# K cache in runs of 32 KB, two heads to a tile: a change to a one-core decode kernel

## The chip, the cores and the metric

The kernel runs on one core of one Trainium2 chip. The metric is the device time of one execution in microseconds (us). A core has five engines that run side by side: TensorE (PE, with its weight loads as PEld), VectorE (DVE), ScalarE (ACT), GpSimd (POOL) and SyncE (SP). SP issues nearly all transfers here, and 16 DMA engines carry them out. On-chip memory (SBUF) has 128 partitions; matmuls write to PSUM.

## The reference

One decode step for 4 sequences (B = 4, one token each, D = 576) is the sum of the input, an attention branch and an MLP branch, both on the layer-normed input:

```
xn = layernorm(x)
out = x + A(xn) + B(xn)

A: q = xn @ wq                          # 32 query heads of 128
   k, v = the last W = 2048 positions of the caches, 16 heads of 128, each used by 2 query heads
   o = softmax(q k^T / sqrt(128)) v
   return o @ wo
B: xn + gelu(layernorm(xn) @ w3) @ w4   # F = 4608; for one token the part before it (h, w1, w2) vanishes
```

With one token, the shifts in branch B move every value out of the sequence, so `w1` and `w2` are not read. All arrays are bf16. The windows of K and V are 4 x 16 x 2048 x 128 values each, 33.55 MB, and with the weights the kernel reads 87.17 MB.

## The kernel before

**Stages.** The kernel works in one pass over its bytes. First come `wq` in five pieces and the query projection (L204), then 16 heads of K, with the five pieces of `w3` between the first of them, then the softmax, then 16 heads of V with the output projections, and at the end three quarters of `w4`.

**K.** `kv_load` (L98) fetches one head for all 4 batches as a tile of 2 MB: 128 partitions (32 blocks of 64 positions x 4 batches), 16 KB of contiguous bytes to each. The pool `kv` has 6 such tiles (`NKV`), and V uses the same pool. `k_scores` (L252) turns the tile around on DVE with two STREAM_TRANSPOSEs (L258), one for each half of the head dimension, into a tile `kt` (a pool of two), and then issues 64 small matmuls (L267), 32 on each half, which add the scores of this head for all batches into four PSUM banks S. The queries lie in `qz` with zeros around them, so that each head's scores land in rows of their own.

**Softmax.** After the last head of K, `softmax` (L273) takes the maximum on DVE (L279), Exp on ACT with four calls of 512 columns, one for each bank (L283), scales and spreads the result (L300, L302), transposes it on PE (L306) and copies it to `PZ` (L312, L314) in four pieces.

**V.** `v_compute` (L319) multiplies one head of V by its columns of `PZ` in 64 matmuls (L325). `head_out` (L342) copies the result out and puts two steps off to later rounds through the list `later`: `select` (L351), and for every second head `project`, eight matmuls with a tile of `wo` (L330). `wo` has a pool of three tiles, loaded by `load_wo` (L338).

**Order.** Each engine takes its instructions in the order written by a scheduler at build time, and waits on semaphores. SP's order decides when a transfer is queued: a transfer that waits for a free buffer holds up all that stand behind it. In the V stage SP has, in this order: V0 to V3, wo0, wo1, V4, wo2, V5, V6, wo3, V7, V8, wo4, and so on. V6 is the first that needs a V buffer back (V0's), and wo3 the first that needs a `wo` buffer back (wo0's, after its `project`). On PE the first two heads of V are computed piece by piece beside each other, as the pieces of `PZ` come; the `project` of wo0 stands behind V3.

Of the kernel before, what the change touches and what calls it, by code (L numbers as in the profile page):

```python
# [8 lines left out]
ACT = mybir.ActivationFunctionType  # L9
ALU = mybir.AluOpType  # L10
AX = mybir.AxisListType
BF16 = mybir.dt.bfloat16
F32 = mybir.dt.float32
I32 = mybir.dt.int32
PSUM = bass.MemoryType.PSUM

NKV = 6
NWP = 3


# [1 line left out]
def kernel(  # L22
# [11 lines left out]
    B_w4: bass.AP,  # L34
    out: bass.AP,
):

    nc = tc.nc
    P = 128
    B, Sq, D = A_x.shape
    _, Hkv, Sk, Dh = A_k_cache.shape
    Hq = A_wq.shape[1] // Dh
    rep = Hq // Hkv
    W = min(4096, max(256, Sk // 4))
    F = B_w3.shape[1]
    assert Sq == 1 and Dh == P and rep == 2 and B == 4 and W == 2048
    assert D == 576 and F % (2 * P) == 0 and Hkv * rep == 32 and Hkv % 2 == 0  # L50
    G = 32
    NCH = W // G
    NG = P // G
    GK = G // B
    NY = 4
# [3 lines left out]
    KJ = 4  # L59
# [4 lines left out]
    scale = float(Dh) ** -0.5  # L64
# [6 lines left out]
    k_win = A_k_cache[:, :, Sk - W:Sk, :]  # L71
    v_win = A_v_cache[:, :, Sk - W:Sk, :]

    def ap_of(t, offset_elems, dims):
        a = t[:]
        return bass.AP(a.tensor, a.offset + offset_elems, [list(a.ap[0])] + [list(d) for d in dims])

    def ap32(t, offset, dims):
        a = t[:].rearrange("p a b -> p (a b)") if len(t.shape) == 3 else t[:].rearrange("p a b c d e -> p (a b c d e)")
        a = a.bitcast(I32)  # L80
        return bass.AP(a.tensor, a.offset + offset, [list(a.ap[0])] + [list(d) for d in dims])

    const = ctx.enter_context(tc.tile_pool(name="const", bufs=1))
    small = ctx.enter_context(tc.tile_pool(name="small", bufs=2))
    kvp = ctx.enter_context(tc.tile_pool(name="kv", bufs=NKV))
    ktp = ctx.enter_context(tc.tile_pool(name="kt", bufs=2))
# [8 lines left out]
    x_bf = const.tile([B, D], BF16)  # L95
    nc.scalar.dma_start(out=x_bf[:], in_=x2)

    def kv_load(win, h):  # L98
        t = kvp.tile([P, NCH, Dh], BF16, tag="kv")
        nc.sync.dma_start(out=t[:].rearrange("p c d -> p (c d)"),  # L100
                          in_=win[:, h].rearrange("b (p c) d -> p b (c d)", p=G))
        return t

    wq_src = A_wq[0:KJ * P, :].rearrange("(p j) n -> p j n", j=KJ)
    w3_src = B_w3[0:KJ * P, :].rearrange("(p j) f -> p j f", j=KJ)
# [4 lines left out]
    def load_rows(src, j, n, name):  # L110
        t = wpl.tile([P, n], BF16, tag="w", name=name)
        nc.sync.dma_start(out=t[:], in_=src[:, j, :])
        return t

    def load_tail(w, n, name):
        t = wpl.tile([P, n // 2], BF16, tag="w", name=name)
        nc.sync.dma_start(out=t[:], in_=w[KJ * P:D, :].rearrange("r (e f) -> (r e) f", e=2))
        return t
# [89 lines left out]
    for j in range(KJ):  # L208
        q_piece(wq_j[j], j)
        if len(wq_j) < KJ:  # L210
            wq_j.append(load_rows(wq_src, len(wq_j), NQ, f"wq{len(wq_j)}"))
    K_tiles = {0: kv_load(k_win, 0)}
    V_tiles = {}

    q_rows = ktp.tile([P, 2, HB, NY, NG, G], BF16, tag="kt", name="q_rows")
# [33 lines left out]

    S = []  # L250

    def k_scores(h):  # L252

        kn = K_tiles.pop(h)

        kt = ktp.tile([P, NCH // 2, 2, G, 2, 2], BF16, tag="kt", name=f"kt{h}")
        for e in range(2):
            nc.vector.transpose(  # L258
                out=ap32(kt, e * G * 2, [[2 * G * 2, NCH // 2], [1, 2], [2, G]]),
                in_=ap32(kn, e * G, [[2 * 2 * G, NCH // 2], [2 * G, 2], [1, G]]))  # L260
        if h == 0:
            S.extend(ps_s.tile([P, 512], F32, tag="S", name=f"S{g}") for g in range(NG))
        for y in range(NY):
            e, t = divmod(y, 2)
            for b in range(B):
                for g in range(NG):
                    nc.tensor.matmul(out=S[g][32 * b:32 * b + 32, :].rearrange("p (c k l) -> p c k l", k=GK, l=2),  # L267
                                     lhsT=qz[32 * g:32 * g + 32, b, h, y, :],
                                     rhs=kt[32 * g:32 * g + 32, :, e, b:G:B, :, t],
                                     start=(h == 0 and y == 0), stop=(h == Hkv - 1 and y == NY - 1),  # L270
                                     skip_group_check=True)

    def softmax():  # L273
        E = wpl.tile([P, NCH, NG, GK], F32, tag="w", name="E")
        mx = const.tile([P, NG], F32)
        nb = const.tile([P, 1], F32)
        sm = const.tile([P, NG], F32)
        for g in range(NG):
            nc.vector.reduce_max(out=mx[:, g:g + 1], in_=S[g][:], axis=AX.X)  # L279
        nc.vector.reduce_max(out=nb[:], in_=mx[:], axis=AX.X)  # L280
        nc.vector.tensor_scalar_mul(out=nb[:], in0=nb[:], scalar1=-scale)  # L281
        for g in range(NG):
            nc.scalar.activation(out=E[:, :, g, :].rearrange("p (c l) k -> p c k l", l=2),  # L283
                                 in_=S[g][:].rearrange("p (c k l) -> p c k l", k=GK, l=2), func=ACT.Exp, bias=nb[:], scale=scale, accum_out=sm[:, g:g + 1])
        rd = const.tile([P, 1], F32)
        nc.vector.tensor_reduce(out=rd[:], in_=sm[:], op=ALU.add, axis=AX.X)
        nc.vector.reciprocal(out=rd[:], in_=rd[:])
        rdm = const.tile([P, B], F32)
        nc.vector.tensor_scalar_mul(out=rdm[:], in0=mask[:], scalar1=rd[:])  # L289

        PZ = pzp.tile([P, NCH, P], BF16, tag="pz", name="PZ")
        HC = CP // 2
        for piece in range(NP):
            c0 = piece * CP
            pr = ktp.tile([P, CP, NG, GK, B], BF16, tag="kt", name=f"pr{piece}")
            for b in range(B):
                src = E[:, c0:c0 + CP, :, :].rearrange("p c g k -> p (c g k)")
                dst = pr[:, :, :, :, b].rearrange("p c g k -> p (c g k)")
                if b == 3 or (b == 1 and piece % 2):
                    nc.scalar.mul(out=dst, in_=src, mul=rdm[:, b:b + 1])  # L300
                else:
                    nc.vector.tensor_scalar_mul(out=dst, in0=src, scalar1=rdm[:, b:b + 1])  # L302
            for half in range(2):
                tp = ps_s.tile([P, HC, P], BF16, tag="S", name=f"pt{piece}{half}")
                for cc in range(HC):
                    nc.tensor.transpose(out=tp[:, cc, :],  # L306
                                        in_=pr[:, half * HC + cc, :, :, :].rearrange("p g k b -> p (g k b)"),
                                        identity=ident[:])
                dst = PZ[:, c0 + half * HC:c0 + (half + 1) * HC, :].rearrange("p c n -> p (c n)")
                src = tp[:].rearrange("p c n -> p (c n)")  # L310
                if half:
                    nc.scalar.copy(out=dst, in_=src)  # L312
                else:
                    nc.vector.tensor_copy(out=dst.bitcast(I32), in_=src.bitcast(I32))  # L314
        return PZ
# [3 lines left out]
    def v_compute(h):  # L319
        bank = ps_o.tile([P, 128], F32, tag="O", name=f"O{h}")  # L320
        O = bank[:, 0:B * rep].rearrange("p (b r) -> p b r", r=rep)
        O_tiles[h] = (O, bank[:, 64:64 + XR * rep * B].rearrange("p (x n) -> p x n", x=XR))
        vn = V_tiles.pop(h)
        for c in range(NCH):
            nc.tensor.matmul(out=O, lhsT=vn[:, c, :], rhs=PZ[:, c, :].rearrange("p (b n) -> p b n", b=B)[:, :, h * rep:(h + 1) * rep],  # L325
                             start=(c == 0), stop=(c == NCH - 1))

    def acc_matmuls(lhsT, rhs_cols):
# [47 lines left out]
    def g_piece(t, j):  # L376
        for fc in range(NF):
            e, i = divmod(fc, NFH)
            if j < KJ:
                lhsT, rhs = t[:, e * (F // 2) + i:(e + 1) * (F // 2):NFH], ln2T[:, j, :]  # L380
            else:
                lhsT, rhs = t[:, i:F // 2:NFH], ln2T[:, KJ + e, :]
            nc.tensor.matmul(out=gp[:, fc, :], lhsT=lhsT, rhs=rhs, start=False, stop=False, skip_group_check=True)  # L383
# [26 lines left out]


    w3 = {}
    for h in range(Hkv):
        if h > 0:
            K_tiles[h] = kv_load(k_win, h)
        if h < KJ:
            w3[h] = load_rows(w3_src, h, F, f"w3_{h}")
        elif h == KJ:
            w3[KJ] = load_tail(B_w3, F, "w3_t")
        k_scores(h)  # L420
        if h in w3:
            g_piece(w3.pop(h), h)
            if h == KJ:
                gelu()


    NV0 = 4
    w4 = load_w4(0, 0, 9, (9,))
    for v in range(NV0):
        V_tiles[v] = kv_load(v_win, v)  # L430
    for g2 in range(2):
        load_wo(g2)
    mlp_out(*w4[0])
# [1 line left out]
    for v in range(Hkv):  # L435
        n = v + NV0
        if n < Hkv:
            V_tiles[n] = kv_load(v_win, n)
            if n % 2 == 0:
                load_wo(n // 2)  # L440
        run_later()
        v_compute(v)
        head_out(v)
# [4 lines left out]
        run_later()  # L448
    for part in end[1:]:
        mlp_out(*part)  # L450
    assert not K_tiles and not V_tiles and not wo_tiles

    fin = const.tile([P, DH], out.dtype)
    NR = 32 + B
# [33 lines left out]
```

## Time and profile before

| What | Value |
|---|---|
| Median of 3 runs | 218.01 us (217.16 to 218.03) |
| Profiled execution, own time | 217.48 us |
| Its span, first to last instruction | 215.6 us |
| Busy: PE, DVE, ACT | 115.0, 108.9, 21.1 us |
| Bytes moved | 87.52 MB, mean 406 GB/s |
| DMA packets | 8255 |
| K: 16 transfers of 2048 KB, issue to landing | 24.7 us (median) |
| V: 16 transfers of 2048 KB, issue to landing | 29.3 us (median) |

The span is what lies between the first and the last instruction of the profiled execution; its own time is 1.9 us longer. A group line of the profile has the source line, the engine, the operation, the tiles written and read, their shapes and the count, then after the first bar the busy time and the mean of one in ns, and after the second the engine's idle time just before these instructions and what ended it. In the row of 40 slices each digit is the busy share in tenths of one 40th of the span. A window line has start and end, its length, the busy time and count of PE, PEld, DVE, ACT and POOL, the granted TensorE clock, the DMA share and GB/s. A line of the chain of waits has start, length and what the chain went through, and a line of SP's waits has total, times and longest.

### The profile page before, as it was taken

To read this page: it belongs to the slowest core of one execution; us is meant where nothing else is said; L and a number is where in the kernel's file an instruction comes from. 1 tells how busy PE (TensorE), PEld (TensorE's weight loads), DVE (VectorE), ACT (ScalarE), POOL (GpSimd) and SP (SyncE) were. 2 spreads that over 40 slices of the span, in tenths; PEclk is the share of its full clock that TensorE was granted. 3 is DMA by queue.
4 is the path that set the end of the run, shared out by engine and by line. 5 is a ranking of instruction groups with operands and counts; after the bars stand their busy time and mean duration, and the time that the engine had idled before them with its cause. 6 is when DMAs were issued, how large, how long until landed. Compare 5 with 4: busy or idle time off the path is not lost.

```text
span 215.6 us, 5534 instructions
## 1 busy us (share of the span) xinstructions
PE 115.0 (53%) x2577; PEld 74.3 (34%) x2577; DVE 108.9 (51%) x156; ACT 21.1 (10%) x36; POOL 1.8 (1%) x8
## 2 busy tenths in 40 slices
PE   0343788748644554445424098748662634536383
PEld 0110744426311111111101087747452434434341
DVE  7932967584999999989785592201100000001000
ACT  0202220000000000000003896100000000000000
POOL 1110000000000000000000000000000000000000
PEclk9999999658767667558588557555555555555559
DMA  6999999999999999999999999999999999999970
GB/s 259 432 418 442 413 436 433 405 439 407 433 426 432 417 423 429 426 429 432 410 438 417 435 411 428 428 417 389 417 430 420 418 433 420 429 422 423 422 288 18
DMA packets 8255, 87.52 MB, mean 406 GB/s; under 512 B 925, under 2 KB 1065, under 8 KB 2729
## 3 DMA queue, kind: packets, MB, share of 16 engines
q1 hardware_dynamic: 8216, 87.17, 96.1%
q8 instruction: 20, 0.33, 0.6%
q14 instruction: 3, 0.02, 0.0%
q10 hardware_dynamic: 16, 0.01, 0.0%
HBM read 87.17 MB, written 0.00 MB: 404 GB/s over the span
## 4 chain that ended last, share of the span: by engine, by line
DMA 70%; DVE 13%; PE 8%; ACT 5%; issue 2%; SPq 1%; DVEq 0%; ACTq 0%
DMA t<-in_A_k_cache_dram 36%; DMA t<-in_A_v_cache_dram 21%; DMA w<-in_B_w_dram 9%; DVE kt L258 6%; DMA wq<-in_A_wq_dram 3%; PE pt L306 3%; PE O L325 2%; ACT E L283 2%; DVE qz L177 2%; PE qp L204 1%; ACT PZ L312 1%; ACT pr L300 1%; DVE mx L279 1%; DVE pr L302 1%; PE ACC L330 1%
## 5 line engine op out<-in xcount | busy, mean ns | idle before, releaser
L258 DVE STREAM_TRANSPOSE kt<-t 128x2048 int32<-128x2048 int32 x32 | 72.3, 2292 | 12.8 <-DMA t<-in_A_k_cache_dram 12.8
L267 PE MATMUL S<-kt,qz 32*32 32x512 bf16 x1024 | 36.9, 625 | 38.0 <-DVE kt L258 36.6
L325 PE MATMUL O<-PZ,t 128*128 128x8 bf16 x1024 | 30.3, 168 | 26.2 <-DMA t<-in_A_v_cache_dram 22.6
L325 PEld LDWEIGHTS <-t 128*128 128x128 bf16 x1024 | 29.0, 104 | 30.2 <-DMA t<-in_A_v_cache_dram 25.2
L347 DVE CAST on<-O 128x8 bf16<-128x8 f32 x16 | 2.7, 167 | 57.9 <-PE O L325 57.8
L267 PEld LDWEIGHTS <-qz 32*32 32x32 bf16 x1024 | 10.8, 94 | 60.6 <-issue 57.4
L306 PE MATMUL pt<-ident,pr 128*128 128x128 bf16 x64 | 6.7, 292 | 9.4 <-DVE pr L302 8.2
L383 PEld LDWEIGHTS <-w 128*128 128x128 bf16 x144 | 9.2, 162 | 5.2 <-DMA w<-in_B_w_dram 2.7
L383 PE MATMUL ACC<-ln2T,w 128*128 128x4 bf16 x144 | 9.6, 202 | 1.7 <-DMA w<-in_B_w_dram 1.7
L330 PE MATMUL ACC<-wo,onx 128*4 128x288 bf16 x64 | 9.0, 436 | 2.2 <-DVE onx L359 2.2
L283 ACT ACTIVATE E<-S,nb 128x512 f32<-128x512 f32 x4 | 4.0, 1115 | 59.5 <-DVE nb L281 59.5
L306 PEld LDWEIGHTS <-pr 128*128 128x128 bf16 x64 | 5.9, 135 | 10.0 <-ACT pr L300 10.0
L300 ACT ACTIVATE pr<-E,rdm 128x512 bf16<-128x512 f32 x6 | 8.1, 1430 | 0.8 <-DVE rdm L289 0.8
L359 DVE CAST onx<-O 32x16 bf16<-32x16 f32 x32 | 5.3, 165 | 5.3 <-PE O L351 4.9
L330 PE MATMUL ACC<-w,gT 128*4 128x288 bf16 x72 | 7.5, 368 | 0.8 <-DMA w<-in_B_w_dram 0.7
L302 DVE TENSOR_SCALAR pr<-E,rdm 128x512 bf16<-128x512 f32 x10 | 6.5, 809 | 0.3 <-PE pt L306 0.2
L204 PE MATMUL qp<-wq,xnT 128*4 128x512 bf16 x32 | 4.0, 620 | 4.5 <-DMA wq<-in_A_wq_dram 4.5
L224 DVE CAST q_rows<-qp 128x256 bf16<-128x256 f32 x8 | 2.9, 410 | 6.4 <-PE qp L204 6.4
L351 PE MATMUL O<-on,ident 128*32 128x8 bf16 x64 | 4.1, 171 | 3.6 <-DVE on L347 3.6
L351 PEld LDWEIGHTS <-ident 128*32 128x32 bf16 x64 | 4.4, 110 | 3.4 <-issue 3.1
L330 PEld LDWEIGHTS <-gT 128*4 128x4 bf16 x72 | 3.9, 104 | 4.7 <-issue 2.1
L330 PEld LDWEIGHTS <-onx 128*4 128x4 bf16 x64 | 3.7, 110 | 4.3 <-DVE onx L359 2.6
(67 smaller groups left out, 51.0 us busy)
## 6 DMA issues: line engine op xcount, KB each, us to landing
t<-in_A_k_cache_dram SPq DMA_DIRECT2D x16, 2048.0 KB, 24.7
t<-in_A_v_cache_dram SPq DMA_DIRECT2D x16, 2048.0 KB, 29.3
w<-in_B_w_dram SPq DMA_DIRECT2D x4, 1152.0 KB, 13.3
wo<-in_A_wo_dram SPq DMA_DIRECT2D x8, 576.0 KB, 21.3
wq<-in_A_wq_dram SPq DMA_DIRECT2D x4, 1024.0 KB, 6.3
w<-in_B_w_dram SPq DMA_DIRECT2D x3, 1296.0 KB, 30.3
w_t<-in_B_w_dram SPq DMA_DIRECT2D x1, 576.0 KB, 14.4
w<-in_B_w_dram SPq DMA_DIRECT2D x1, 576.0 KB, 25.1
```

The source lines that it names most:

```text
L204: nc.tensor.matmul(out=qp[k][32 * i:32 * i + B, :], lhsT=lhsT, rhs=rhs, start=False, stop=False, skip_group_check=True)
L258: nc.vector.transpose(out=ap32(kt, e * G * 2, [[2 * G * 2, NCH // 2], [1, 2], [2, G]]), in_=ap32(kn, e * G, [[2 * 2 * G, NCH // 2], [2 * G ...
L267: nc.tensor.matmul(out=S[g][32 * b:32 * b + 32, :].rearrange("p (c k l) -> p c k l", k=GK, l=2), lhsT=qz[32 * g:32 * g + 32, b, h, y, :], ...
L283: nc.scalar.activation(out=E[:, :, g, :].rearrange("p (c l) k -> p c k l", l=2), in_=S[g][:].rearrange("p (c k l) -> p c k l", k=GK, l=2), ...
L300: nc.scalar.mul(out=dst, in_=src, mul=rdm[:, b:b + 1])
L302: nc.vector.tensor_scalar_mul(out=dst, in0=src, scalar1=rdm[:, b:b + 1])
L306: nc.tensor.transpose(out=tp[:, cc, :], in_=pr[:, half * HC + cc, :, :, :].rearrange("p g k b -> p (g k b)"), identity=ident[:])
L325: nc.tensor.matmul(out=O, lhsT=vn[:, c, :], rhs=PZ[:, c, :].rearrange("p (b n) -> p b n", b=B)[:, :, h * rep:(h + 1) * rep], start=(c == 0 ...
L330: nc.tensor.matmul(out=ACC[32 * q:32 * q + B, 0:DH], lhsT=lhsT, rhs=rhs_cols(q * DH, (q + 1) * DH), start=False, stop=False, skip_group_ch ...
L351: nc.tensor.matmul(out=T[0:32, x, :], lhsT=ident[:, x:P:XR], rhs=on[:].rearrange("p r b -> p (r b)"), start=(x == 0), stop=(x == XR - 1), ...
L359: nc.vector.tensor_copy(out=onx[q:q + 32, :, :], in_=T[0:32, :, r * B:(r + 1) * B])
L383: nc.tensor.matmul(out=gp[:, fc, :], lhsT=lhsT, rhs=rhs, start=False, stop=False, skip_group_check=True)
```

## The change

K is loaded for two heads at a time, `hp` and `hp + 8`, in one tile of 4 MB (`k_load`): 16 blocks of 128 positions x 8 pairs of batch and head half, so that each partition gets 32 KB of contiguous bytes. The pool `kv` has three tiles of 4 MB where it had six of 2 MB. The two heads share the 128 partitions, so `k_scores` now makes four transposes for a pair, and the two `kt` tiles hold one half of the head dimension each, for both heads; 128 matmuls follow, 64 on each `kt`. The columns of S hold another order of positions, and so Exp is called eight times on 256 columns, and its sums have eight columns where there were four. V keeps runs of 16 KB: two heads share a 4-MB tile, and each head is a transfer of its own into its half (`v_load`). The loop over K takes two pieces of `w3` in each of its first two rounds, and `w3_t` in the third.

In the built order SP has wq_t, wq0, wq1, K pair 0, wq2, wq3, w3_0, w3_1, K pair 1, w3_2, w3_3, K pair 2, w3_t, K pairs 3 to 7, w4's first part, V0 to V3, wo0, wo1, V4, wo2, V5, V6, wo3, V7, V8 and so on. On PE the `project` of wo0 now stands behind V2, ahead of V3. V6's buffer is free when V0 and V1 are both done, V8's when V2 and V3 are.

```diff
--- before.py
+++ after.py
@@ -14,7 +14,7 @@
 I32 = mybir.dt.int32
 PSUM = bass.MemoryType.PSUM
 
-NKV = 6
+NKV = 3
 NWP = 3
 
 
@@ -76,7 +77,7 @@
         return bass.AP(a.tensor, a.offset + offset_elems, [list(a.ap[0])] + [list(d) for d in dims])
 
     def ap32(t, offset, dims):
-        a = t[:].rearrange("p a b -> p (a b)") if len(t.shape) == 3 else t[:].rearrange("p a b c d e -> p (a b c d e)")
+        a = t[:].rearrange("p a b -> p (a b)") if len(t.shape) == 3 else t[:].rearrange("p a b c d -> p (a b c d)")
         a = a.bitcast(I32)
         return bass.AP(a.tensor, a.offset + offset, [list(a.ap[0])] + [list(d) for d in dims])
 
@@ -95,11 +96,22 @@
     x_bf = const.tile([B, D], BF16)
     nc.scalar.dma_start(out=x_bf[:], in_=x2)
 
-    def kv_load(win, h):
-        t = kvp.tile([P, NCH, Dh], BF16, tag="kv")
+    def kv_tile():
+        return kvp.tile([P, 2 * NCH, Dh], BF16, tag="kv", name="kv")
+
+    def k_load(hp):
+        t = kv_tile()
+        src = k_win.rearrange("b (x h) s d -> h (b x) s d", x=2)[hp]
         nc.sync.dma_start(out=t[:].rearrange("p c d -> p (c d)"),
-                          in_=win[:, h].rearrange("b (p c) d -> p b (c d)", p=G))
+                          in_=src.rearrange("y (q c) d -> q y (c d)", q=16))
         return t
+
+    def v_load(h):
+        if h % 2 == 0:
+            V_tiles[h] = kv_tile()
+        t = V_tiles[h - h % 2]
+        nc.sync.dma_start(out=t[:, (h % 2) * NCH:(h % 2 + 1) * NCH, :].rearrange("p c d -> p (c d)"),
+                          in_=v_win[:, h].rearrange("b (p c) d -> p b (c d)", p=G))
 
     wq_src = A_wq[0:KJ * P, :].rearrange("(p j) n -> p j n", j=KJ)
     w3_src = B_w3[0:KJ * P, :].rearrange("(p j) f -> p j f", j=KJ)
@@ -209,7 +221,7 @@
         q_piece(wq_j[j], j)
         if len(wq_j) < KJ:
             wq_j.append(load_rows(wq_src, len(wq_j), NQ, f"wq{len(wq_j)}"))
-    K_tiles = {0: kv_load(k_win, 0)}
+    K_tiles = {0: k_load(0)}
     V_tiles = {}
 
     q_rows = ktp.tile([P, 2, HB, NY, NG, G], BF16, tag="kt", name="q_rows")
@@ -249,41 +261,53 @@
 
     S = []
 
-    def k_scores(h):
-
-        kn = K_tiles.pop(h)
-
-        kt = ktp.tile([P, NCH // 2, 2, G, 2, 2], BF16, tag="kt", name=f"kt{h}")
+    def k_scores(hp):
+
+        kn = K_tiles.pop(hp)
+        NC2 = 2 * NCH
+
+        kts = []
         for e in range(2):
-            nc.vector.transpose(
-                out=ap32(kt, e * G * 2, [[2 * G * 2, NCH // 2], [1, 2], [2, G]]),
-                in_=ap32(kn, e * G, [[2 * 2 * G, NCH // 2], [2 * G, 2], [1, G]]))
-        if h == 0:
+            kt = ktp.tile([P, NC2 // 2, G, 2, 2], BF16, tag="kt", name=f"kt{hp}_{e}")
+            for i in range(2):
+                nh = NC2 // 4
+                nc.vector.transpose(
+                    out=ap32(kt, i * nh * 2 * G, [[2 * G, nh], [1, 2], [2, G]]),
+                    in_=ap32(kn, i * nh * 4 * G + e * G, [[4 * G, nh], [2 * G, 2], [1, G]]))
+            kts.append(kt)
+        if hp == 0:
             S.extend(ps_s.tile([P, 512], F32, tag="S", name=f"S{g}") for g in range(NG))
         for y in range(NY):
             e, t = divmod(y, 2)
-            for b in range(B):
-                for g in range(NG):
-                    nc.tensor.matmul(out=S[g][32 * b:32 * b + 32, :].rearrange("p (c k l) -> p c k l", k=GK, l=2),
-                                     lhsT=qz[32 * g:32 * g + 32, b, h, y, :],
-                                     rhs=kt[32 * g:32 * g + 32, :, e, b:G:B, :, t],
-                                     start=(h == 0 and y == 0), stop=(h == Hkv - 1 and y == NY - 1),
-                                     skip_group_check=True)
+            for x in range(2):
+                for b in range(B):
+                    for g in range(NG):
+                        nc.tensor.matmul(
+                            out=S[g][32 * b:32 * b + 32, :].rearrange("p (c k l) -> p c k l", k=GK // 2, l=2),
+                            lhsT=qz[32 * g:32 * g + 32, b, hp + Hkv // 2 * x, y, :],
+                            rhs=kts[e][32 * g:32 * g + 32, :, 2 * b + x:G:2 * B, :, t],
+                            start=(hp == 0 and y == 0 and x == 0),
+                            stop=(hp == Hkv // 2 - 1 and y == NY - 1 and x == 1), skip_group_check=True)
 
     def softmax():
-        E = wpl.tile([P, NCH, NG, GK], F32, tag="w", name="E")
+        E2 = wpl.tile([P, NCH * G], F32, tag="w", name="E")
+        E = E2[:].rearrange("p (c g k) -> p c g k", g=NG, k=GK)
         mx = const.tile([P, NG], F32)
         nb = const.tile([P, 1], F32)
-        sm = const.tile([P, NG], F32)
+        sm = const.tile([P, 2, NG], F32)
         for g in range(NG):
             nc.vector.reduce_max(out=mx[:, g:g + 1], in_=S[g][:], axis=AX.X)
         nc.vector.reduce_max(out=nb[:], in_=mx[:], axis=AX.X)
         nc.vector.tensor_scalar_mul(out=nb[:], in0=nb[:], scalar1=-scale)
-        for g in range(NG):
-            nc.scalar.activation(out=E[:, :, g, :].rearrange("p (c l) k -> p c k l", l=2),
-                                 in_=S[g][:].rearrange("p (c k l) -> p c k l", k=GK, l=2), func=ACT.Exp, bias=nb[:], scale=scale, accum_out=sm[:, g:g + 1])
+
+        for i in range(2):
+            for g in range(NG):
+                nc.scalar.activation(
+                    out=ap_of(E2, i + GK * g, [[2 * G, NCH // 2], [2, GK // 2], [G, 2]]),
+                    in_=S[g][:, i * 256:(i + 1) * 256].rearrange("p (c k l) -> p c k l", k=GK // 2, l=2),
+                    func=ACT.Exp, bias=nb[:], scale=scale, accum_out=sm[:, i, g:g + 1])
         rd = const.tile([P, 1], F32)
-        nc.vector.tensor_reduce(out=rd[:], in_=sm[:], op=ALU.add, axis=AX.X)
+        nc.vector.tensor_reduce(out=rd[:], in_=sm[:].rearrange("p i g -> p (i g)"), op=ALU.add, axis=AX.X)
         nc.vector.reciprocal(out=rd[:], in_=rd[:])
         rdm = const.tile([P, B], F32)
         nc.vector.tensor_scalar_mul(out=rdm[:], in0=mask[:], scalar1=rd[:])
@@ -320,9 +344,9 @@
         bank = ps_o.tile([P, 128], F32, tag="O", name=f"O{h}")
         O = bank[:, 0:B * rep].rearrange("p (b r) -> p b r", r=rep)
         O_tiles[h] = (O, bank[:, 64:64 + XR * rep * B].rearrange("p (x n) -> p x n", x=XR))
-        vn = V_tiles.pop(h)
+        vn, c0 = V_tiles[h - h % 2], (h % 2) * NCH
         for c in range(NCH):
-            nc.tensor.matmul(out=O, lhsT=vn[:, c, :], rhs=PZ[:, c, :].rearrange("p (b n) -> p b n", b=B)[:, :, h * rep:(h + 1) * rep],
+            nc.tensor.matmul(out=O, lhsT=vn[:, c0 + c, :], rhs=PZ[:, c, :].rearrange("p (b n) -> p b n", b=B)[:, :, h * rep:(h + 1) * rep],
                              start=(c == 0), stop=(c == NCH - 1))
 
     def acc_matmuls(lhsT, rhs_cols):
@@ -410,24 +434,22 @@
 
 
     w3 = {}
-    for h in range(Hkv):
-        if h > 0:
-            K_tiles[h] = kv_load(k_win, h)
-        if h < KJ:
-            w3[h] = load_rows(w3_src, h, F, f"w3_{h}")
-        elif h == KJ:
-            w3[KJ] = load_tail(B_w3, F, "w3_t")
-        k_scores(h)
-        if h in w3:
-            g_piece(w3.pop(h), h)
-            if h == KJ:
+    for hp in range(Hkv // 2):
+        if hp > 0:
+            K_tiles[hp] = k_load(hp)
+        for j in range(2 * hp, min(2 * hp + 2, KJ + 1)):
+            w3[j] = load_rows(w3_src, j, F, f"w3_{j}") if j < KJ else load_tail(B_w3, F, "w3_t")
+        k_scores(hp)
+        for j in sorted(w3):
+            g_piece(w3.pop(j), j)
+            if j == KJ:
                 gelu()
 
 
     NV0 = 4
     w4 = load_w4(0, 0, 9, (9,))
     for v in range(NV0):
-        V_tiles[v] = kv_load(v_win, v)
+        v_load(v)
     for g2 in range(2):
         load_wo(g2)
     mlp_out(*w4[0])
@@ -435,7 +457,7 @@
     for v in range(Hkv):
         n = v + NV0
         if n < Hkv:
-            V_tiles[n] = kv_load(v_win, n)
+            v_load(n)
             if n % 2 == 0:
                 load_wo(n // 2)
         run_later()
@@ -448,7 +470,7 @@
         run_later()
     for part in end[1:]:
         mlp_out(*part)
-    assert not K_tiles and not V_tiles and not wo_tiles
+    assert not K_tiles and not wo_tiles
 
     fin = const.tile([P, DH], out.dtype)
     NR = 32 + B
```

## Prediction

> **What bounds the kernel now.** I read the page first: busy shares, the 40 slices, the split of the chain that ended last.
>
> ```profile
> PE 115.0 (53%) x2577; PEld 74.3 (34%) x2577; DVE 108.9 (51%) x156; ACT 21.1 (10%) x36; POOL 1.8 (1%) x8
> DMA  6999999999999999999999999999999999999970
> ...
> DMA 70%; DVE 13%; PE 8%; ACT 5%; issue 2%; SPq 1%; DVEq 0%; ACTq 0%
> ...
> L258 DVE STREAM_TRANSPOSE kt<-t 128x2048 int32<-128x2048 int32 x32 | 72.3, 2292 | 12.8 <-DMA t<-in_A_k_cache_dram 12.8
> L283 ACT ACTIVATE E<-S,nb 128x512 f32<-128x512 f32 x4 | 4.0, 1115 | 59.5 <-DVE nb L281 59.5
> ```
>
> No engine is busy for much over half of the span, while the 16 DMA engines are full in every slice but the first and the last two. So time can change in two ways only: the bytes flow at another rate, or the queue runs dry. Hence the windows, for the K stage and for the one stretch that dips:
>
> ```profile
> 24.00:28.00 4.00, 2.54 (x24) 1.91 (x22) 3.79 (x9) 1.40 (x6) 0.00 (x0) 1.00 0.97 402
> 60.00:104.00 44.00, 20.32 (x576) 5.83 (x576) 40.72 (x19) 0.00 (x0) 0.00 (x0) 0.66 1.01 427
> 144.00:148.00 4.00, 3.92 (x84) 3.29 (x84) 0.38 (x3) 0.00 (x0) 0.00 (x0) 0.50 0.92 351
> ```
>
> The last two columns are DMA share and GB/s: 427 while K streams, 351 at 144 to 148, where the queue is almost empty. Why there, the chain in order of time and SP's waits tell:
>
> ```profile
> 108.23 4.52 DVE kt L258 x2
> ...
> 112.78 1.23 PE S L267 x31
> 114.01 2.48 DVE mx L279 x4
> ...
> 116.95 4.06 ACT E L283 x8
> ...
> 135.46 0.57 PE O L325 x16
> ...
> 145.20 0.33 SPq L338
> ...
> 191.29 20.30 DMA w<-in_B_w_dram
> ```
> ```profile
> SPq L338 <- PE ACC L330: 19.5, 4, 8.7
> SPq L100 <- PE O L351: 17.6, 3, 15.3
> ```
>
> The last K tile lands at 108.1. From there to the end of V0 and V1 (136.03, computed interleaved) there is a serial softmax, and the buffers hold no more than V0 to V5. SP waits 15.3 us for V0's buffer (V6), then 8.7 us for the first output projection (wo3, with V7 behind it), and goes on at 145.20. That is the kernel's weak spot.
>
> **How dry it is, by engine.** The trace's DMA packet records hold a 4-byte mark per engine at each transfer's end. V5's marks run from 140.8 to 144.4 (nine engines by 142.5), V6's from 145.7 to 148.4. After the issue at 145.20 the first packet starts at 146.2, so issue to data is 1.0 us; about half of the engines idled 0.2 to 0.7 us. The time is set by the last engine: an undisturbed one needs 66.1 us from V6's first packet to its end at 207.4, others end as late as 211.5, and then come 0.68 us of matmuls, 0.45 of `fin` and the store. The spread comes from 16-KB instruction fetches, 20 in all, 8 after 146, each of which stops one engine for about 1.05 us.
>
> **The change part by part.** The profiled execution took 217.48 us, 215.6 of span and 1.9 around it; it lies 0.53 below the median of 218.01.
>
> *Runs of 32 KB.* The bytes are the same. A 16-KB packet takes 613 ns in the records, an 8-KB one 309: doubling a run saves 5 ns. Each engine has 64 packets fewer, 0.3 us at best. No row shows a 32-KB packet; the bound on the other side is the slowest full stretch while K streams, 402 GB/s instead of 427, which makes 33.55 MB 4.9 us longer. I take 0, the packet rows being the nearest.
>
> *K0 is 4 MB and lies ahead of wq2 and wq3.* 2.1 MB more, 4.9 us at 427 GB/s, so q comes at about 25 instead of 20.2. What hides it is DVE's slack: it idled 12.8 us for K in the stage, and its first pair need be done only when the second lands, at about 40 by the byte order. Cost 0; with the cover gone up to 4.9. In SP's new order w3_1 stands ahead of K1 and w3_3 ahead of K2, each behind a matmul piece that ends some 2 us or more before the queue would be empty.
>
> *A pool of three pairs.* Four transposes are 9.1 us, a pair's load is 9.8. Pair h+3 is issued when pair h is transposed; h+1 is then landing and h+2 still to come, about 9 us of cover. Cost 0.
>
> *The end of K.* The last pair has the same bytes ahead of it as K15, so it lands at 108.1 too, but now four transposes follow and not two: +4.51. Behind the last one come 64 score matmuls and not 32 (one kt tile holds half of Dh for both heads): 1.13 more. Exp becomes eight calls of 256 columns. Four of 512 took 4.06, 0.98 each with the accumulator's read (208 ns). If columns alone counted, nothing is added; if a half cost a whole, 3.9. A 256-column ACT cast took 375 ns and the read 208, so near 0.6 with the overlap seen: I take +1.0. Together the softmax is late by 6.6 us, bounds 5.6 to 9.5.
>
> *V in pairs.* Each head waits for its own transfer, as before. V6's tile is free when V0 and V1 are both done, which costs nothing since they end together, now at 136.03 + 6.6 = 142.6. In the new order of PE the first projection stands right behind V2, ahead of V3, so wo3 and V7 are issued near 146.5, while V6 still streams until 148.5: no second hole (with the old place it would be 151.8, and a hole of some 4 us). V8 waits for V3 (149 to 151) with V7 in the queue.
>
> *Sum.* V6's first packets come at 143.65. The fast engines, done with V5 at 140.8, idle 2.8 us (before: 0.5); the slowest, at 144.1 to 144.4, idle nothing. So the hole is eaten mostly by engines that had time to spare: undisturbed ones now end at 143.65 + 66.1 = 209.75, the slowest at 210.5 and more, and with one or two fetches behind it the last ends at about 211.9 instead of 211.5: +0.4. With 6.6 replaced by 5.6 it is about 0, by 9.5 it is +2.2 to +3.2. Forecast: 217.48 + 0.4 = 217.9 as a profiled run, 218.4 as a median.
>
> **Rivals.** A difference under 0.5% (1.1 us) is about what a measurement here cannot tell from none.
>
> *The hole reaches the slowest engines (slower).* Place: V6's issue. Price: once V6's data come after 144.4 no engine has work, and each further us is a us of the kernel. It decides from a softmax delay of 7.4. For it: the Exp bound alone gives 9.5; PE sat 2.51 us on "issue" at 140.75, and the same ahead of V1's end would be enough. Against: the nearest ACT rows say 1.0, and that idle time lay in V3. At 9.5: 217.48 + 2.7 + 0.5 = 220.7.
>
> *K streams more slowly.* The source is now walked as 16 runs for each of 8 places (4 batches, 2 head halves) 16.8 MB apart; before, 4 places 33.6 MB apart. If engines in step then read places that collide, the K stage falls towards 402 GB/s: 218.4 + 4.9 = 223.3. Against: 33.6-MB steps cost nothing visible at 427. [...]
>
> *K streams faster.* If larger runs lift K to 447 GB/s, the best stretch in the windows (20 to 24), 33.55 MB take 3.5 us less: 214.9. Against: the 613 and 309 ns. [...]
>
> *The change doesn't do what it says.* If a 32-KB run goes out as two 16-KB packets, only the transfer term is zero for sure, and the time is the forecast's.
>
> **How the numbers follow.** Forecast (hole mostly hidden, packet split or not) 0.52, of it 0.06 slower by over 0.5% and 0.03 faster; dry queue 0.22, all slower; slow K 0.14, nearly all slower; fast K 0.12, of it 0.03 within the bound. Faster 0.12, same 0.47, slower 0.41. The forecast's own range is 217.4 to 219.4; the low end of 216.4 and the high end of 222.0 reach into fast K and slow K and leave out about 0.1 on each side.
>
> **What would show it.** Right: K packets of 32 KB near 1.22 us; the last pair's four transposes from about 108.2 to 117.3; Exp in 5 us; V0 and V1 done near 142.6; a dip in GB/s between 141 and 144 and none after; last DMA landing near 212. Wrong: K below 420 or above 435 GB/s between 60 and 104; a wait of DVE for K that grows pair by pair; a second hole before V7; or a dip of two slices, with all engines idle.

## The result and the profile after

The changed kernel takes 299.62 us (median of 6 runs, 297.76 to 301.44) against 217.83 us before: a ratio of 1.3763, interval 1.3702 to 1.3824. The forecast was 218.4 us in a range up to 222.0. Its profiled execution took 299.94 us with a span of 297.9.

The page first: busy shares, the DMA rows of the 40 slices, the split of the chain that ended last, and the groups of the transposes and of Exp.

```profile
PE 110.5 (37%) x2577; PEld 79.0 (27%) x2577; DVE 108.1 (36%) x156; ACT 21.6 (7%) x44; POOL 1.8 (1%) x8
...
DMA  7999999899999999999999999999998999999992
GB/s 298 266 211 227 420 302 211 181 354 213 211 240 203 216 213 216 202 227 220 213 211 211 209 211 191 350 433 429 414 427 357 435 420 419 430 418 423 424 415 79
...
DMA 58%; DVE 16%; PE 10%; another core or an unknown queue 8%; ACT 4%; issue 4%; SPq 0%; DVEq 0%; ACTq 0%
...
L274 DVE STREAM_TRANSPOSE kt<-kv 128x2048 int32<-128x2048 int32 x32 | 71.4, 2284 | 83.6 <-DMA kv<-in_A_k_cache_dram 83.6
L305 ACT ACTIVATE E<-S,nb 128x256 f32<-128x256 f32 x8 | 4.5, 702 | 106.1 <-DVE nb L301 106.1
...
kv<-in_A_k_cache_dram SPq DMA_DIRECT2D x8, 4096.0 KB, 48.9
```

The engines do the work of before in the time of before (DVE 108.1 us, was 108.9). DVE's wait for K went from 12.8 to 83.6 us. The row of busy tenths still shows 9 in all but four of the 40 slices: the DMA engines were hardly ever out of work. But the row below it shows about 211 GB/s (191 to 240) wherever K alone is in the queue, up to 420 where `w3` is and 414 to 435 once V begins, but for one slice of 357. So here a busy DMA share does not say that bytes flow at full rate.

The windows of the changed kernel (start and end, length, engines, granted clock, DMA share, GB/s) put two stages side by side, and give the stretch that the prediction named, 60 to 104:

```profile
60.00:104.00 44.00, 14.82 (x364) 10.92 (x365) 19.37 (x14) 0.32 (x1) 0.00 (x0) 0.50 1.01 237
128.00:136.00 8.00, 1.85 (x64) 1.02 (x64) 6.41 (x3) 0.00 (x0) 0.00 (x0) 0.50 1.03 217
192.00:200.00 8.00, 3.87 (x103) 1.98 (x118) 7.13 (x4) 0.00 (x0) 0.00 (x0) 0.50 1.01 431
```

The line from 128 lies in K, the one from 192 in V; both have a full DMA share, one half of the rate of the other. The stretch from 60 has some `w3` in it beside K. In the packet records (a packet here is one run: 1024 of 32 KB for the eight pairs of K) a 32-KB packet of K took 2526 ns at the median (the forecast had 1.22 us) and a 16-KB packet of V 613 ns, as before. The last five K pairs land 19.8 to 20.1 us apart at the median engine, and not 9.8.

The chain, in order of time, shows where the time was lost:

```profile
118.80 49.95 DMA kv<-in_A_k_cache_dram
...
190.24 0.10 DVE kt L274
192.48 6.67 DVE kt L274 x3
199.19 2.03 PE S L285 x58
201.21 2.48 DVE mx L299 x4
...
204.15 4.56 ACT E L305 x16
```

The transposes of the last pair start at 190.24; before, those of the last head started at 108.23. That is 82.0 us later. From there to the end of the span it is 107.7 us (297.9 - 190.24), before 107.4 (215.6 - 108.23). The whole loss lies in the loading of K. By rates alone, 33.55 MB at 212 instead of 427 GB/s are 158.3 instead of 78.6 us: 79.7 us more.

### The profile page after: what moved, and what is told of

Read it like the earlier page. It is cut to its first block, busy times and chain, and to the rows that moved or that the text cites. A ratio compares the mean times of both kernels' runs of the same rounds, so it can differ in the third digit from the quotient of the medians.

```text
span 297.9 us, 5523 instructions
## 1 busy us (share of the span) xinstructions
PE 110.5 (37%) x2577; PEld 79.0 (27%) x2577; DVE 108.1 (36%) x156; ACT 21.6 (7%) x44; POOL 1.8 (1%) x8
## 4 chain that ended last, share of the span: by engine, by line
DMA 58%; DVE 16%; PE 10%; another core or an unknown queue 8%; ACT 4%; issue 4%; SPq 0%; DVEq 0%; ACTq 0%
DMA kv<-in_A_k_cache_dram 33%; DMA w<-in_B_w_dram 19%; DVE kt L274 10%; DMA wo<-in_A_wo_dram 6%; PE ACC L354 3%; PE O L349 3%; ACT E L305 2%; PE pt L330 1%; DVE qz L189 1%; ACT pr L324 1%; ACT PZ L336 1%; PE qp L216 1%; DVE mx L299 1%; PE ACC L407 1%
## 5 line engine op out<-in xcount | busy, mean ns | idle before, releaser
L274 DVE STREAM_TRANSPOSE kt<-kv 128x2048 int32<-128x2048 int32 x32 | 71.4, 2284 | 83.6 <-DMA kv<-in_A_k_cache_dram 83.6
L285 PE MATMUL S<-kt,qz 32*32 32x512 bf16 x1024 | 31.6, 608 | 76.2 <-DVE kt L274 76.2
L285 PEld LDWEIGHTS <-qz 32*32 32x32 bf16 x1024 | 15.8, 97 | 89.7 <-issue 86.8
L349 PE MATMUL O<-PZ,kv 128*128 128x8 bf16 x1024 | 30.3, 168 | 19.9 <-DMA kv<-in_A_v_cache_dram 18.5
L349 PEld LDWEIGHTS <-kv 128*128 128x128 bf16 x1024 | 28.9, 104 | 23.7 <-DMA kv<-in_A_v_cache_dram 20.9
L354 PE MATMUL ACC<-w,gT 128*4 128x288 bf16 x72 | 8.7, 408 | 13.9 <-DMA w<-in_B_w_dram 13.9
L305 ACT ACTIVATE E<-S,nb 128x256 f32<-128x256 f32 x8 | 4.5, 702 | 106.1 <-DVE nb L301 106.1
L407 PE MATMUL ACC<-ln2T,w_t 128*128 128x4 bf16 x36 | 2.4, 202 | 14.4 <-DMA w_t<-in_B_w_dram 14.4
L216 PEld LDWEIGHTS <-xnT 128*4 128x4 bf16 x40 | 1.1, 101 | 21.8 <-issue 21.5
L407 PEld LDWEIGHTS <-w_t 128*128 128x128 bf16 x36 | 2.3, 162 | 14.5 <-DMA w_t<-in_B_w_dram 14.5
```

Source lines behind the costliest of these rows:

```text
L216: nc.tensor.matmul(out=qp[k][32 * i:32 * i + B, :], lhsT=lhsT, rhs=rhs, start=False, stop=False, skip_group_check=True)
L274: nc.vector.transpose(out=ap32(kt, i * nh * 2 * G, [[2 * G, nh], [1, 2], [2, G]]), in_=ap32(kn, i * nh * 4 * G + e * G, [[4 * G, nh], [2 * ...
L305: nc.scalar.activation(out=ap_of(E2, i + GK * g, [[2 * G, NCH // 2], [2, GK // 2], [G, 2]]), in_=S[g][:, i * 256:(i + 1) * 256].rearrange( ...
L349: nc.tensor.matmul(out=O, lhsT=vn[:, c0 + c, :], rhs=PZ[:, c, :].rearrange("p (b n) -> p b n", b=B)[:, :, h * rep:(h + 1) * rep], start=(c ...
L354: nc.tensor.matmul(out=ACC[32 * q:32 * q + B, 0:DH], lhsT=lhsT, rhs=rhs_cols(q * DH, (q + 1) * DH), start=False, stop=False, skip_group_ch ...
```

## The experiments

Three things in K's transfer changed together: the length of a run (32 instead of 16 KB), the places it reads (eight places 16.8 MB apart), and the order of its rows over the partitions (16 blocks of 8 rows, where it was 32 blocks of 4). A row is one run, and it fills one partition; "16 x 8 rows" means that row j of block i goes to partition 8i + j (with 32 x 4 rows to 4i + j). The first experiment times the transfer by itself, with nothing computed.

**Nine kinds of load, alone.**

```diff
+    # s2: runs of 32 KB, two heads, all batches (as after)
...
+    # s3: the same places in two transfers with runs of 16 KB
...
+    # s4: runs of 32 KB, one piece of 4 MB
...
+        nc.sync.dma_start(out=t[:], in_=flat(i * 2097152, [[16384, P], [1, 16384]]))
```

> Loads alone, nine kinds one after the other, each byte read from the K cache; the computation is left out (the output is the input x with a few values of the tiles in it). In the changed kernel a 32-KB packet took 2526 ns in the median where two of 16 KB take 1226, so K came at about 211 GB/s. Theory 'length': a packet well over 16 KB is slow wherever it lies. Then the kinds with runs of 32 KB (s2, s4, s5) all give about 211 GB/s and s7 and s8 (24 and 18 KB) lie in between or at 211, while s1, s3, s6, s9 (16 KB) give about 427. Theory 'places': the engines, in step, read places 32 KB apart or 16.8 MB apart that collide. Then s2 and s3 (same places, runs of 32 and of 16 KB) both give about 211, s5 (32 KB, 36 KB apart) and s7, s8 give about 427, and s6 (16 KB, 32 KB apart) tells whether the 32-KB pitch alone does it: about 211 if so, 427 if it is the 16.8 MB steps.

Measured, from the packet records:

| Load | ns a packet | GB/s |
|---|---|---|
| 16 KB, 32 x 4 rows (as before) | 611 | 420 to 431 |
| 32 KB, 16 x 8 rows (as after) | 2547 | 209 to 213 |
| the same places, two transfers of 16 KB | 1264 | 214 |
| 32 KB, 128 rows of one piece of 4 MB | 1218 | 432 |
| 32 KB, 128 rows 36 KB apart | 1218 | 432 |
| 16 KB, 128 rows 32 KB apart | 615 | 428 |
| 24 KB, 128 rows | 916 | 431 |
| 18 KB, 128 rows | 691 | 429 |
| 16 KB, 128 rows of one piece of 2 MB | 615 | 428 |

Length is not it: 32-KB runs from one piece go at 432 GB/s, and with 16-KB runs from the changed kernel's places the rate is still 214. I took this for proof that the places decide. It was none, because every fast load from other places had other rows as well, 32 x 4 or 128 even ones.

**The changed kernel with two transfers of 16-KB runs to a pair.** Rows and places stay as in the change.

```diff
+        src = src.rearrange("y (q z c) d -> z q y (c d)", q=16, z=2)
+        for z in range(2):
+            nc.sync.dma_start(out=t[:, z * NCH:(z + 1) * NCH, :].rearrange("p c d -> p (c d)"), in_=src[z])
```

> The changed kernel with one edit: each pair of K is fetched by two transfers of 2 MB in runs of 16 KB into the two halves of the same tile, so places, tile layout, pool and all computation stay as in the changed kernel. Theory 'length': K is back at 427 GB/s and the time falls to what the prediction forecast for everything else, 218 to 219 us. Theory 'places': still near 300 us. Apart from the loads the prediction's sum can be read here: softmax later by 6.6 us (5.6 to 9.5), V6 issued near 142.6, end about 0.4 us later than before.

293.3 us, ratio to before 1.3498 (1.3411 to 1.3585). Between 100 and 155 us the 16-KB packets took 1231 ns at the median, half of them 1054 to 1274. The run length is cleared in the kernel itself too.

**Which distances hurt?** Loads alone, 16-KB runs, 16 x 8 rows with ten sets of distances, and one load of 32 x 4 rows.

```diff
+    # u1: 16 x 32 KB, 8 x 16 MB
...
+    # u4: 16 x 32 KB, 8 x (16 MB + 4 KB)
...
+    # u9: 16 x 32 KB, 8 x 512 KB
...
+    # u10: 32 x 16 KB, 4 x 32 MB
```

> Loads alone, all in runs of 16 KB and of 2 MB each, as 16 x 8 (or 32 x 4) rows; only the distances of the rows differ, and the computation is left out. m1 gave 214 GB/s for the changed kernel's places and 428 to 432 for every other kind, whatever its run. Theory 'same low address': engines that read at one moment from places whose addresses differ by a large power of two share one path into memory. If the rows go round the engines in turn (row 0 to engine 0, row 1 to engine 1, ...), the kernel before has 4 such places at a time (full rate) and the changed one 8 (half), so one path would give about 107 GB/s, four engines' worth. Then: u1 213, u10 427; u2 (same kind of places, but 8 neighbouring rows in one place) about 427; u3 (16 MB + 512 KB) 427; u11 (16 places 4 MB apart at a time) near 107; u5 213, and from u6 to u9 (4 MB, 2 MB, 1 MB, 512 KB) the rate comes back to 427 somewhere, at the latest in u9. If instead each engine has neighbouring rows, u2 is the slow one, 107 to 213. Theory 'far steps': a large step from row to row costs time in itself, whatever the low address: u3 and u4 stay at 213, and u2, whose steps are mostly 32 KB, is fast. u4 (16 MB + 4 KB) tells whether 4 KB are enough to part the places.

No distance mattered. Every load of 16 x 8 rows took 1267 to 1269 ns a packet, 212 GB/s, from 16 MB down to 512 KB, with 4 KB or 512 KB added, and even where the 128 runs lie evenly, 32 KB apart, in one piece of 4 MB. The load of 32 x 4 rows, with the largest distance of all, took 615 ns, 428 GB/s. Both theories on the places fell.

**The changed kernel, K read as 128 rows of 32 KB.** All else is as changed. It reads other positions of the cache.

```diff
-        src = k_win.rearrange("b (x h) s d -> h (b x) s d", x=2)[hp]
+        kf = A_k_cache[:]
+        src = bass.AP(kf.tensor, kf.offset + hp * 2 * NCH * Dh * P, [[2 * NCH * Dh, P], [1, 2 * NCH * Dh]])
-                          in_=src.rearrange("y (q c) d -> q y (c d)", q=16))
+                          in_=src)
```

> The changed kernel with one edit: each pair's 4 MB are read from one piece of the K cache (runs of 32 KB, one behind the other) instead of from 8 places 16.8 MB apart. The tile, the run, the pool, the order and all computation are those of the changed kernel; the values are those of other positions and heads. Theory 'places': K flows at 430 GB/s, and the time shows what all the rest of the change costs: by the prediction's sum 217.9 as a profiled run, 218.4 as a median (softmax 6.6 us later, bounds 5.6 to 9.5; V6 issued near 142.6; a hole between 141 and 144 that the slowest engines do not see). Theory 'length' has fallen in m1, and would give about 300 us. If something else in the changed kernel also costs tens of us, the time stays well above 222.

216.96 us against 217.32, ratio 0.9977 (0.9966 to 0.9987). Its windows line for the same stretch as shown of before, then its chain:

```profile
60.00:104.00 44.00, 17.43 (x576) 9.09 (x576) 40.78 (x25) 0.32 (x1) 0.00 (x0) 0.50 1.00 429
```
```profile
105.89 0.10 DVE kt L275
105.99 2.14 issue
108.13 6.67 DVE kt L275 x3
...
114.84 2.02 PE S L286 x64
116.86 2.49 DVE mx L300 x4
...
119.80 4.56 ACT E L306 x16
...
138.81 0.18 DVE on L372
...
190.23 20.31 DMA w<-in_B_w_dram
```

K streams at 429 GB/s in packets of 1215 ns. The rest of the change (pool of three, four transposes, eight Exp calls, V in pairs, the new order) costs nothing that lasts, and so the forecast's other steps can be judged on this run. It also shows what was to be won: with K at full rate the change gains 0.2%. No run reads the right positions in 32-KB runs at full rate; another order of their rows was not tried.

**The kernel before, only K's rows as 16 x 8.** Still 2-MB tiles and 16-KB runs; other positions of the cache are read.

```diff
+        if win is k_win:
+            kf = A_k_cache[:]
+            n = NCH * Dh
+            src = bass.AP(kf.tensor, kf.offset + h * 2 * P * n, [[2 * n, 16], [32 * n, 8], [1, n]])
```

'Ports' and 'shape' are two theories on the row order: the rate goes by which partitions are written at the same time, or by the numbers of the shape alone.

> The kernel before with one edit: K's transfers, 2 MB in runs of 16 KB, are 16 x 8 rows (runs 32 KB apart, 8 places 512 KB apart, inside one piece of 4 MB for each head) and not 32 x 4; the values are those of other positions. Nothing else of the change is in it. Theories 'ports' and 'shape' alike: K falls to 212 GB/s, 16 heads take 158 us instead of 79, and the time is near 217.4 + 79 = 296 us; with f3 (216.96 us with all the rest of the change) the shape would then be the whole of the loss. If it stays near 217, the changed kernel's loss needs something else of the change as well.

296.1 us (median of four runs), ratio 1.3567 (1.3461 to 1.3673, without the longest run of 298.93 us). The stretch that was at 427 GB/s:

```profile
60.00:104.00 44.00, 11.73 (x296) 7.08 (x296) 18.09 (x14) 0.32 (x1) 0.00 (x0) 0.54 1.01 228
```

With this run the cause is bracketed from both sides: the row shape makes the old kernel slow, and the new kernel without it is fast. Both runs also read other places, but the loads alone had shown that the places cost nothing (16 x 8 rows took 1267 to 1269 ns at every distance).

**Why the shape? Which partitions are written at once.** Loads alone, 16-KB runs: three full shapes, and loads of four packets each to 8 single partitions (w4 to w8) or 16 (w9, w10). In the DMA row of this run's page, 4 to 5 tenths of the 16 engines are busy in the loads to 8 partitions, 7 to 9 tenths in those to 16, but for the end of the last.

```diff
+    # w4: 8 partitions, 4 apart
...
+        nc.sync.dma_start(out=t[0:29:4, 0:32768].rearrange('p (r n) -> p r n', r=4), in_=src)
...
+    # w5: 8 partitions, 1 apart
...
+        nc.sync.dma_start(out=t[0:8:1, 0:32768].rearrange('p (r n) -> p r n', r=4), in_=src)
```

> Loads alone in runs of 16 KB, computation left out. m2 left both theories of the source's addresses fallen: 16 x 8 rows gave 212 GB/s whatever their distances, even inside one piece of 4 MB, and 32 x 4 rows 428. What is left is the shape of the transfer. [...] Theory 'shape': the rate goes by the numbers of the shape alone (8 rows to an engine in one block are slow to read or to set up), wherever the partitions lie: w4 to w8 all alike, w9 and w10 alike.

| Load | ns a packet |
|---|---|
| 32 x 4 rows; 64 x 2 rows | 611; 615 |
| 16 x 8 rows | 1243 |
| 8 partitions, 4 apart | 611 |
| 8 partitions, 2, 8 or 16 apart | 1279, 1291, 1295 |
| 8 partitions, 1 apart | 2413 |
| 16 partitions, 4 apart | 1300 |
| 16 partitions, 1 apart | 2413 |

A packet's time goes by which partitions are written at the same time: with 8 of them 611 ns where they lie 4 apart, 1279 to 1295 (about twice) where they lie 2, 8 or 16 apart, and 2413 (about four times) where they lie 1 apart. The theory 'shape', which had w4 to w8 alike and w9 and w10 alike, falls. Whether the partitions explain the three full shapes too depends on which engine takes which rows, and the trace does not say that.

**Partitions by pairs.** Loads with few engines; a1, a2 and a3 are 4 x 8, 8 x 8 and 2 x 8 rows.

```diff
+    # a1: 4 x 8 rows, partitions 0 to 31
...
+    # a4: partitions 0 and 1
...
+    # a5: partitions 0 and 4
...
+    # a6: partitions 0 and 32
...
+    # a7: partitions 0 and 64
```

> Loads alone, computation left out; few engines at a time, so that it shows who shares with whom. All in packets of 16 KB but the last two kinds. In m4 and m5 engines that were put half a transfer, or 8 us, behind gained nothing, which speaks against 'in step'. [...] Theory 'block of eight' (rows of one engine that lie in eight neighbouring partitions are slow as such): a1, a2 and a3 all 1220.

Partitions 0 and 1 took 1291 ns a packet, 0 and 32 took 1297; 0 and 4 took 612, 0 and 64 took 611. One engine alone took 121 ns for 3 KB to partition 0 and to 96 alike. 4 x 8 rows took 611, so a block of eight rows is not slow as such; 8 x 8 rows took 619 at the median with a tail up to 1093. In that load four of the engines were late from the load before (their transfers ended 2.3 us after the others'), which matters below.

**Does it hang on the engines being in step?** If engines slow each other only while they write such partitions (0 and 32, say) at the same moment, some of those that are half a transfer out of step would be faster. Which rows an engine takes no record shows, so this was a guess. Two runs put some engines behind (x1 and x3 are the transfers ahead of the lag and behind it):

```diff
+    # x2: four engines get 4 packets of 16 KB more
...
+    nc.sync.dma_start(out=lag[0:13:4, :].rearrange('p (r n) -> p r n', r=4), in_=flat(0, [[65536, 4], [16384, 4], [1, 8192]]))
```

> Loads alone, computation left out: five transfers of 16 x 8 rows, then one small transfer of 4 x 4 runs of 16 KB that only four engines carry, then five transfers of 16 x 8 rows again. [...] Theory 'shape' (blocks of eight rows are slow in themselves, for some reason that no run has shown): x3 as x1, all near 1260.

> As m4, computation left out, but only one engine is put behind. [...] Here five transfers of 16 x 8 rows (y1), a transfer of 17 runs of 6 KB that one engine carries, five of 16 x 8 (y3), one of 17 runs of 1 KB on one engine, five of 16 x 8 (y5). [...]

Neither gave the fast packets. With four engines 4.9 us behind, 93% of the packets stayed between 1090 and 1275 ns and a transfer took 9.55 instead of 9.8 us. With one engine 8.1 us behind none was under 1100; behind the second, smaller lag of that run about 1% were.

**From rest.** Every group of transfers now starts with all engines idle; the lag goes to four engines, and pairs of transfers are issued from one queue or from two. The question is whether the moment counts at which the engines write, or a limit common to all sixteen engines, as theory B has it.

```diff
+    # c2: 8 x 8 rows
...
+    # c6: four engines behind, 8 x 8 rows
...
+    # c7: 16 x 4 rows on SP's queue, then 16 x 4 rows on SP's queue
...
+    # c9: 16 x 8 rows on SP's queue, 16 x 8 rows on ACT's queue
```

> Loads alone, runs of 16 KB, and each group of transfers starts with all engines idle, so the engines start together. [...] Theory B (a limit common to all sixteen engines that the shape meets, no matter who is in step): 8 x 8 rows 0.61 from rest and behind the lag; 16 x 8 rows 1.22 in every way of issuing them, behind a lag or from two queues too, and 16 x 4 rows 0.61.

| Load | median ns a packet, three times |
|---|---|
| 16 x 8 rows | 1236, 1255, 1255 |
| 8 x 8 rows | 1203, 1214, 1232 |
| 32 x 4 rows | 611, 611, 611 |
| 8 x 8 rows, four engines behind | 727, 713, 703 |
| 16 x 8 rows, one engine behind | 1224, 1236, 1219 |
| 16 x 8 rows, four engines behind | 1227, 1221, 1222 |
| 16 x 4 rows twice, one queue | 1240, 1264, 1221 |
| 16 x 4 rows twice, two queues | 1217, 1204, 1238 |
| 16 x 8 rows twice, two queues | 1169, 1174, 1172 |

For 8 x 8 rows the moment counts: they are slow from rest (1203 to 1232 ns, where theory B had 0.61 us), and mostly fast when four engines are late (703 to 727; about 40% of the packets under 640 ns, some 70% under 900, the lag's included). 16 x 4 rows, to 64 partitions each, are slow too, at 1204 to 1264 ns; theory B had them at 0.61 us. For all sixteen engines B's words fit better: lateness (1219 to 1236 ns) and a second queue (1169 to 1174) gained little against 1236 to 1255. So that 16 x 8 rows lose half of the rate by which partitions are written at the same time is argued from the smaller loads and not shown. Why sixteen engines do not get out of each other's way as eight do is open; the trace does not name the engine of a packet, so which rows each engine takes could not be read.

## Why the prediction was wrong, point by point

- **The step that failed: "Runs of 32 KB ... I take 0".** It put the cost of the transfer at nothing, by the length of a packet alone, and its bound on the other side, 402 GB/s from the slowest full stretch, could not contain a factor of two. Measured: packets of 2526 ns where 1.22 us were forecast, and the last pair's transposes 82.0 us later. What cost it is the order of the rows over the partitions, since the same 32-KB runs in even rows cost nothing (216.96 us against 217.32). The length term itself was right: where the rows are 128 even ones, a 32-KB packet takes 1215 to 1218 ns against 2 x 613, and with 64 packets fewer on each engine that is some 0.6 us gained. What the step never asked was in which order the rows go to partitions. The sentence on the source, "16 runs for each of 8 places", described the rows that did it, and only its address side was weighed.
- **The rival "K streams more slowly" had the place, not the mechanism and not the price.** Colliding places priced at 402 GB/s gave 223.3 us. The distances had no effect at all in the loads alone (1267 to 1269 ns from 512 KB to 16 MB). The sign named as wrong, K under 420 GB/s between 60 and 104 with DVE waiting pair by pair, is what came: 237 GB/s over that stretch, 83.6 us of waits.
- **K0 ahead of wq2 and wq3, the pool of three.** Cost 0 holds. In the run with even rows K came at 429 GB/s between 60 and 104, and DVE waited 9.6 us for K in all, less than the 12.8 of before.
- **The end of K.** The last pair's four transposes took 8.9 us from first to last, 4.4 more than the two of before (forecast 4.51); the matmuls behind them 2.02 against 1.23, +0.8 (forecast 1.13); Exp 4.56 against 4.06, +0.5 (forecast 1.0; a call of 256 columns takes 0.70). V0 and V1 were done 138.99 - 105.89 = 33.1 us after the transposes began, before 136.03 - 108.23 = 27.8: a delay of 5.3 us, where the forecast had 6.6 with bounds 5.6 to 9.5, just below the lower. They were done at 138.99 by the clock, where the forecast had 142.6: 1.3 us of that is the smaller delay, and 2.3 us come from transposes that began at 105.89 and not at 108.2.
- **No second hole.** Right, and by the new place of the first projection: wo0's matmuls end at 142.72, ahead of V3's, and wo3 goes out at 142.75. SP's waits in the run with even rows (total, times, longest), then a window:

```profile
SPq L114 <- PE O L376: 30.1, 5, 19.5
SPq L363 <- PE O L376: 3.2, 1, 3.2
```
```profile
136.00:144.00 8.00, 7.04 (x178) 6.39 (x176) 2.18 (x10) 1.01 (x1) 0.00 (x0) 0.52 0.99 407
```

  V6 waits longer for its buffer (19.5 us, was 15.3), but wo3's wait behind it shrank from 8.7 to 3.2 us. The first hole hardly came either: V6 was issued at 139.02 and not near 142.6, and where the forecast had a dip between 141 and 144 the queue stayed full (DMA share 0.99). So the fast engines' 2.8 us of idle time in the forecast's sum did not come.
- **The sum of the rest.** Forecast +0.4 us, measured -0.36 us at the medians and -0.84 us in the profiled runs, so the sign was missed. In these two profiles K's marks (the records at a transfer's end) come 0.5 us earlier at the median engine (104.9 instead of 105.4), about what the longer packets gain, and the slowest engine's 1.9 earlier, since before one engine was late at K's end; and the softmax delay was smaller. The rival "the hole reaches the slowest engines" did not happen: its point was a delay of 7.4 us, and 5.3 came.

## What to carry to other kernels

When a transfer's row order changes, work out which on-chip partitions are written at the same time, and not only how long the runs are and where they lie. Here 32 x 4, 64 x 2 or 128 even rows reached full rate (420 to 432 GB/s), while 16 x 8 rows halved it (209 to 221); in the smaller loads a packet's time goes by which partitions are written at the same time (0 and 1: 1291 ns, 0 and 4: 612), and that is the likely, not the shown, reason. A DMA share of 1.0 does not rule out such a loss (1.03 at 217 GB/s here): read GB/s and the time of one packet beside it, and measure a new shape alone before building on it.

## What the runs showed of the hardware

- Row shape alone halves a load: 16 x 8 rows 209 to 221 GB/s in a steady row of transfers, with runs of 16 as of 32 KB; 32 x 4 and 64 x 2 rows (runs of 16 KB) and 128 rows (16 to 32 KB) 420 to 432.
- A 16-KB packet's time goes by which partitions are written together. 0 and 1: 1291 ns, 0 and 32: 1297, 0 and 4: 612, 0 and 64: 611. Eight partitions 4 apart: 611, 2, 8 or 16 apart: 1279 to 1295, 1 apart: 2413. Sixteen 4 apart: 1300, 1 apart: 2413.
- In 128 even rows, packets beyond 16 KB gain little and lose nothing: 16 KB 615, 18 KB 691, 24 KB 916, 32 KB 1218 ns, each 26.6 to 26.9 GB/s.
- Two queues did not lift the rate: 16 x 8 rows from SP's and ACT's queues together moved 214 to 218 GB/s.
